# Attention, top-1 experts and FFN on one core: where the routing of three token batches stands among the heads

## The chip, the cores and the metric

One core of a Trainium2 chip runs the whole program. The metric is the device time of one execution in microseconds (us). TensorE (PE), VectorE (DVE), ScalarE (ACT) and GpSimd (POOL) each work through their own list of instructions in order; SyncE (SP) issues most loads and stores. An engine that waits holds up all that stands behind it in its list.

## The reference

Three layers over 4 × 576 = 2304 tokens in fp32: causal attention mixed with a memory read-out (8 heads of 64), a mixture of 8 experts of which each token takes one, and a dense FFN with ELU.

```python
# attention, per batch b and head h
a = softmax(causal(q @ k.T / 8)); local = a @ v
q_p = elu(q) + 1
mem = (q_p @ M_prev) / (q_p @ z_prev + 1e-6)
x = g * mem + (1 - g) * local            # g = sigmoid(beta); heads side by side: 512 wide
# experts
logits = x @ w_gate + modality_bias[modality_id]
e = argmax(logits); gate = softmax(logits)[e]
y = gate * (relu(x @ w1[e]) @ w2[e])     # 512 -> 1024 -> 512
# FFN
out = elu(y @ w_in) @ w_out              # 512 -> 2048 -> 512
```

## The kernel before

Attention runs over 16 pairs of heads (p = 0 to 15; four pairs are one batch of 576 tokens), each in 7 units (k = 0 to 6) of score tiles. One loop walks all units: it issues the scores of a unit on TensorE and then whatever `put(p, k, ...)` has hung on that unit: transposed weights, products with v, the memory's products, loads. So the order of each engine's list is written out by hand, by the numbers of `put` and the constants at the head of the file.

Small VectorE work isn't hung on a unit directly but queued, and `pump()`, called after each scores' minimum, each copy of transposed weights and each step of the feature map, lets out one entry of `steps` and one of `slow` (two of `slow` from the last batch of this loop on, `rate`). `steps` takes a pair's finishing: reciprocals, scaling, and `fin(p)` (L586), which adds memory and local part: four additions a pair, of the main rows (128 x 4 x 128), of the last 64 rows of the batch (`xt`, 64 x 128), and of the two tiles of logits that were computed beside them (widths 8 instead of 64). A batch has 576 = 4 × 128 + 64 tokens; the 64 of an even batch lie in the lower half of `xt`'s partitions, those of an odd batch in the upper half (`rows.start` is 64). L606 sends an addition to VectorE from pair 13 on, or where the rows are the upper half; all others go to GpSimd.

`slow` takes the routing. Tokens are routed in groups of 9, 4 and 5 tiles of 128 (`GROUPS`). For each: `logits` sums the heads' logits, `soft` takes maximum and exponential, `choose` makes the one-hot `oh` and its running sum `r_up` on VectorE and then three products on TensorE (L678 to L680, `tri` and `ones` against `oh` and `r_up`) that count how many tokens of each expert stand before a token; `gates` makes the gate and stores the rows to `xd` in DRAM; `place_a` and `place_b` turn counts into places (`rpi`); `route_d` scatters token numbers to these places in the list `idreg`, by one indirect DMA of GpSimd per tile (L94). `RY` empty entries stand between `choose` and `gates`.

The first two groups are routed in the loop of heads. The first expert is then known; its weights are loaded and split into a high and a low part (`wsplit`, L882 on ScalarE and L883), and `gather0(0)` fetches the first block of 256 rows (`xb`) by the list so far. In the loop's last part stand `scale` (the gate times the rows, L902 on ScalarE and L903 on VectorE) at unit 10 after the last pair's start and `turn` (8 transposes on TensorE, L912, and the split of the result) at unit 13. Block 0 follows: 8 hidden tiles of 12 products (L929), then 4 × 24 products to the output (L948). The last group is routed inside block 0: `logits`, `soft`, `choose` behind hidden tile 0 (`RA`), `gates`, the placements and the five scatters behind tile 2 (`RB`). After hidden tile 7 tables of the experts' counts are made, the second block's list is loaded (`gi`, L886) and its rows are gathered (L888); then 18 scatters fill `idc`, the list of the rows of all later blocks.

Of the kernel before, what the change touches and what calls it, by code (L numbers as in the profile page):

```python
# [10 lines left out]
F32 = mybir.dt.float32  # L11
# [11 lines left out]
E, FF = 8, 1024  # L23
# [3 lines left out]
BLK = 256  # L27
# [27 lines left out]
FINV = 13  # L55
# [5 lines left out]
GB = 7  # L61
EL = (7, 7)
ML = (7, 7)
RA = 0
RB = 2
GK = (5, 5, 5)
SY = 4
RY = 4
# [1 line left out]
MW = (7, 7, 8, 8)  # L70
WSP = (2, 3, 6, 7)
WEN = 'pppp'
SC0 = 10
TU = (13, 13)
H1 = ()
PRE0 = (2, 4)

CD, CQ, CH, CX = S, S + 128, S + 640, S + 768
# [136 lines left out]
def attention(tc, G, ap, hd):  # L215
# [372 lines left out]
    def fin(p):  # L588
        b, hp = p // 4, p % 4
        xs, xt = XS[b % 2], XT[b // 2]  # L590
        if hp == 0:
            nc.gpsimd.memset(xs[:, :, DM + 1 : ROW], 0.0)
            if b % 2 == 0:
                nc.gpsimd.memset(xt[:, DM + 1 : ROW], 0.0)
        c0 = 128 * hp
        mm, ol = MM[p % 2], OL[p % 2]
        r = 64 * (b % 2)
        hs = slice(2 * hp, 2 * hp + 2)
        half = slice(r, r + 64)
        for out, rows, c, d in (  # L600
            (xs[:, :, c0 : c0 + 128].rearrange("p c (j d) -> p c j d", d=64), slice(0, 128), slice(0, 4), slice(0, D)),
            (xt[half, c0 : c0 + 128].rearrange("p (j d) -> p j d", d=64), half, 4, slice(0, D)),
            (LX[:, :, hs], slice(0, 128), slice(0, 4), slice(D, DL)),
            (LT[b // 2][half, hs], half, 4, slice(D, DL)),
        ):
            if p >= FINV or rows.start:  # L606
                steps.append(lambda out=out, rows=rows, c=c, d=d: nc.vector.tensor_tensor(out, mm[rows, c, :, d], ol[rows, c, :, d], op=ALU.add))
            else:
                nc.gpsimd.tensor_tensor(out, mm[rows, c, :, d], ol[rows, c, :, d], op=ALU.add)
# [49 lines left out]
    def choose(t0, K):  # L659
        eq = wk.tile([128, 9, E], F32, tag="r_eq", bufs=1, name=f"r_eq{t0}")[:, :K]  # L660
        fm = wk.tile([128, 9, 1], F32, tag="r_fm", bufs=1, name=f"r_fm{t0}")[:, :K]
        up = wk.tile([128, E * 9], F32, tag="r_up", bufs=1, name=f"r_up{t0}")[:, : E * K]
        L, mxl, O = lg[:, t0 : t0 + K, :], G.gm[:, t0 : t0 + K], oh[:, t0 * E : (t0 + K) * E]
        Oe = O.rearrange("p (e c) -> p e c", e=E)
        nc.vector.tensor_tensor(eq, L, mxl.to_broadcast([128, K, E]), op=ALU.is_equal)
        yield
        nc.vector.tensor_tensor(eq, eq, revE.unsqueeze(1).to_broadcast([128, K, E]), op=ALU.mult)
        yield
        nc.vector.tensor_reduce(fm, eq, axis=AX.X, op=ALU.max)
        yield  # L670
        nc.vector.tensor_tensor(Oe, fm[:, :, 0].unsqueeze(1).to_broadcast([128, E, K]), revE.unsqueeze(2).to_broadcast([128, E, K]), op=ALU.is_equal)
        yield

        nc.vector.tensor_tensor_scan(out=up, data0=G.go[:, t0 * E : (t0 + K) * E], data1=O, initial=0.0, op0=ALU.mult, op1=ALU.add)
        yield
        pt = s(f"r_ps{t0}")[:, 0 : 10 * E]
        pl, al = RT[t0, "pt"] = pt[:, 0 : E * K], pt[:, E * K : E * K + E]
        nc.tensor.matmul(pl, tri, O, start=True, stop=False)  # L678
        nc.tensor.matmul(pl, ones, up, start=False, stop=True)
        nc.tensor.matmul(al, ones, up[:, K - 1 :: K], start=True, stop=True)  # L680
        yield
# [70 lines left out]
    def put(p, k, f, *a):  # L752
        beside.setdefault(NU * p + k, []).append((f, a))
# [41 lines left out]
    for b, (t0, K) in enumerate(((0, 0), (0, 9), (9, 4))):  # L795
# [7 lines left out]
        put(p, k, slow.append, iter((None,) * RY))  # L803
        put(p, k, slow.append, gates(b))
        if K:
            put(p, k, slow.append, place_a(t0, K))
            if b == 2:
                put(p, k, slow.append, first_expert())
# [17 lines left out]
        put(NP - 1, WSP[q], lambda q=q: G.wsplit(0, 0, q, WEN[q], G.RAW0[q]))  # L826
    put(NP - 1, EAR, early)
    put(NP - 1, EAR, lambda: G.gather0(0))
    put(NP - 1, SC0, lambda: G.first_rows())
    put(NP - 1, SC0, lambda: G.scale(G.XB[0]))  # L830
    put(NP - 1, W2L, second_loads)
    put(NP - 1, TU[0], drain)
    for a in range(2):
        put(NP - 1, TU[a], lambda a=a: G.turn(G.XB[0], (a,), G.X0, s))
    for f, k in enumerate(H1):
        put(NP - 1, k, lambda f=f: G.hidden(0, f, G.X0))


    def first_prep(n):
# [15 lines left out]
    while steps or slow:  # L855
        pump()

    ts = range(13, 18)
    G.last_batch = dict(ts=ts, logits=logits(3), soft=soft(3), choose=choose(13, 5), gates=gates(3), place_a=place_a(13, 5), place_b=place_b(13, 5), route_d=route_d)


def define_experts(tc, G):
# [137 lines left out]

def experts(tc, G, mp):
    nc, ct = tc.nc, G.ct
    L = G.last_batch
    oh, rk, run, iotE, cpi = G.oh, G.rk, G.run, G.iotE, G.cpi
    wload, wsplit, gather0, gather1, scale, turn, block = G.wload, G.wsplit, G.gather0, G.gather1, G.scale, G.turn, G.block
    t8 = lambda n: ct(n, [128, E])
# [55 lines left out]
    def start_of(u, j):  # L1062
        return nc.values_load(nxti[0:1, u, j : j + 1], engines=[mybir.EngineType.SP], min_val=0, max_val=NTOK, **why)

    ts = L["ts"]
    P = lambda f, *a: (lambda: f(*a))
    R_ = lambda n: (lambda: deque(L[n], maxlen=0))
    mid1 = {
        RA: [R_("logits"), R_("soft"), R_("choose")],
        RB: [R_("gates"), R_("place_a"), R_("place_b")] + [P(L["route_d"], t) for t in ts],  # L1070
    }
    mid2 = {0: [G.late_T], 1: []}

    def early_load(q):
# [14 lines left out]
    mid2.setdefault(EB[0], []).append(P(early_bits, 0))  # L1089
    mid2.setdefault(EB[1], []).append(P(scale, G.XB[1]))  # L1090
    mid2.setdefault(TX, []).append(P(turn, G.XB[1]))
    block(0, slice(0, BLK), mid1, mid2, len(H1), G.X0)
    W[2][0] = G.kp.tile([128, 4096], F32R, tag="k1", name="W20")
    load_eid(1)
    gather0(2)
# [385 lines left out]
```

## Time and profile before

| | |
|---|---|
| time, median of 3 runs | 971.13 us (970.19 to 972.72) |
| the profiled execution | 980.77 us, of which its span 979.0 |
| mean granted clock of TensorE | 0.95 of full |
| TensorE busy | 891.9 us (91%) |
| VectorE, ScalarE, GpSimd busy | 554.2, 486.6, 279.8 us |
| attention up to its last output product | 258.74 us of the span |
| block 0 and what follows, experts, FFN | from there to 979 us |

How to read it: TensorE is busy nearly always, so time is lost where it isn't, or where it runs at a lower granted clock. The rows further down give busy times by stretches of the span; where a stretch ends with a pair of heads, it is the start of that pair's last product with v (L522).

### The profile page before, as it was taken

How to read it: one execution, taken by the hardware profiler on the slowest of the kernel's cores; microseconds unless marked ns; L12 is line 12 of the kernel's file. 1: busy time of each engine (PE TensorE's matmuls, PEld its weight loads, DVE VectorE, ACT ScalarE, POOL GpSimd, SP SyncE). 2: the span in 40 equal slices, each digit the busy share in tenths (PEclk: the TensorE clock that was granted, in tenths of full speed). 3: DMA queues.
4: the chain of work that ended last, by engine and by line, in shares of the span. 5: the costliest groups of instructions: out<-in, count | busy, mean ns of one | idle time of the engine just before them, and what ended most of it. 6: DMA issues, size and time to landing. Idle time of an engine off the chain costs nothing. (4 is left out here: it accounts for less than half of the span.)

```text
span 979.0 us, 16337 instructions
## 1 busy us (share of the span) xinstructions
PE 891.9 (91%) x6038; PEld 801.3 (82%) x6038; DVE 554.2 (57%) x1280; ACT 486.6 (50%) x1141; POOL 279.8 (29%) x405
## 2 busy tenths in 40 slices
PE   6999988789687899889997689999999999999996
PEld 4887776677676899889995488999999999999995
DVE  7789886688663432244221379888554444644442
ACT  4577765465421222233112365666766666665553
POOL 6443322724326330001100033222332222322223
PEclk7899998898897899989998889999999999999998
DMA  7122322524316160042011033431010000100001
GB/s 185 50 82 85 128 63 102 59 57 143 108 56 159 15 216 23 4 130 88 24 30 36 10 131 134 148 122 72 11 55 1 1 1 1 66 1 1 1 1 64
DMA packets 29553, 65.14 MB, mean 67 GB/s; under 512 B 11008, under 2 KB 11136, under 8 KB 29440
## 3 DMA queue, kind: packets, MB, share of 16 engines
q1 hardware_dynamic: 23520, 49.50, 17.1%
q0 software_dynamic: 4832, 12.14, 4.0%
q10 hardware_dynamic: 1088, 2.10, 0.6%
q8 instruction: 58, 0.95, 0.5%
q14 instruction: 55, 0.45, 0.2%
HBM read 54.14 MB, written 9.58 MB: 65 GB/s over the span
## 5 line engine op out<-in xcount | busy, mean ns | idle before, releaser
L1331 POOL TENSOR_TENSOR gl<-eg,gh 128x384 fp32r<-128x384 f32 x86 | 94.2, 1096 | 274.5 <-PE fh L1312 186.6
L1342 PE MATMUL facc<-wl,gh 128*128 128x512 f32 x288 | 112.6, 391 | 1.0 <-POOL wl L1292 1.0
L1342 PE MATMUL facc<-wh,gl 128*128 128x512 f32 x288 | 112.6, 391 | 0.0
L1342 PE MATMUL facc<-wh,gh 128*128 128x512 f32 x288 | 112.3, 390 | 0.0
L948 PE MATMUL acc<-hs,W 128*128 128x256 f32 x864 | 107.3, 283 | 2.3 <-issue 1.3
L929 PE MATMUL h<-xh,W 128*128 128x256 f32 x512 | 97.4, 292 | 12.6 <-issue 9.1
L948 PEld LDWEIGHTS acc<-hs,W 128*128 128x128 f32 x864 | 104.2, 189 | 3.2 <-ACT hs L931 1.1
L1312 PE MATMUL fh<-yh,first_w 128*128 128x384 f32 x384 | 100.2, 342 | 5.7 <-ACT yh L1303 5.7
L1319 ACT ACTIVATE er<-fh 128x384 f32<-128x384 f32 x96 | 47.2, 492 | 113.1 <-PE fh L1312 110.2
L1322 DVE SCALAR_TENSOR_TENSOR ee<-ee,er 128x384 f32<-128x384 f32 x48 | 27.9, 580 | 120.2 <-ACT er L1321 118.7
L455 ACT ACTIVATE sr<-sr,mx 128x512 f32<-128x512 f32 (+3 forms) x128 | 71.8, 563 | 46.3 <-DVE mx L404 43.7
L929 PEld LDWEIGHTS h<-xh,W 128*128 128x128 f32 x512 | 83.3, 199 | 13.2 <-issue 9.4
L931 ACT ACTIVATE hs<-h 128x256 fp32r<-128x256 f32 x72 | 27.3, 385 | 118.8 <-PE h L929 101.5
L385 POOL TENSOR_TENSOR heads<-lqk,heads 128x704 fp32r<-128x704 f32 (+1 forms) x31 | 46.1, 1488 | 122.9 <-ACT heads L382 107.9
L888 POOL DMA_INDIRECT xb<-xd,gi x26 | 25.3, 973 | 190.1 <-ACT xh L913 77.8
L1312 PEld LDWEIGHTS fh<-yh,first_w 128*128 128x128 f32 x384 | 71.5, 192 | 7.8 <-ACT yh L1303 5.2
L404 DVE CUSTOM_DVE_ANT_0 sr<-s,mb 128x512 f32<-128x512 f32 (+2 forms) x144 | 69.8, 504 | 12.5 <-PE s L436 5.4
L929 PE MATMUL h<-xl,W 128*128 128x256 f32 x256 | 75.0, 293 | 0.3 <-issue 0.3
L932 DVE SCALAR_TENSOR_TENSOR hs<-h,hs 128x256 fp32r<-128x256 f32 x72 | 30.1, 423 | 72.4 <-ACT hs L931 67.0
L489 DVE COPY aT<-t 128x512 f32<-128x512 f32 (+3 forms) x106 | 49.9, 481 | 30.5 <-PE t L477 28.5
L1312 PE MATMUL fh<-yh,wh 128*128 128x384 f32 x192 | 64.5, 336 | 0.9 <-DVE eg L1323 0.9
L1312 PE MATMUL fh<-yh,wl 128*128 128x384 f32 x192 | 64.4, 336 | 0.1
(343 smaller groups left out, 2019.1 us busy)
## 6 DMA issues: line engine op xcount, KB each, us to landing
raw<-in_w_dram SPq DMA_DIRECT2D x20, 512.0 KB
lqk<-in_qk_dram SPq DMA_DIRECT2D x15, 672.0 KB
fraw<-in_win_dram SPq DMA_DIRECT2D x14, 512.0 KB
fraw<-in_wout_dram SPq DMA_DIRECT2D x14, 512.0 KB
vt<-in_vP_dram SPq DMA_DIRECT2D x16, 320.0 KB
xd<-early_rows SPq DMA_DIRECT2D x2, 1032.0 KB
xd<-late_rows SPq DMA_DIRECT2D x2, 1032.0 KB
raw<-in_w_dram ACTq DMA_DIRECT2D x4, 512.0 KB
```

Of the source, the lines that this page charges most:

```text
L385: eng.tensor_tensor(heads[:, p % 2, 1, PART[n]], LD[p % 2][:, PART[n]], heads[:, p % 2, 0, PART[n]].bitcast(F32), op=ALU.subtract)
L404: nc.vector.tensor_tensor_reduce(out=dst, in0=src, in1=mask, scale=-0.125, scalar=start, op0=ALU.add, op1=ALU.min, accum_out=least)
L455: nc.scalar.activation(sr[:, o : o + W], sr[:, o : o + W], AF.Exp, scale=-1.0, bias=mx[:, r : r + 1], accum_out=SUM[p][:, i, j : j + 1])
L489: nc.vector.tensor_copy(dst, src)
L929: nc.tensor.matmul(hp, wt[:, k, 128 * f : 128 * f + 128], xt[:, k, :], start=(k == 0 and r == 0), stop=(k == 3 and r == 2))
L932: nc.vector.scalar_tensor_tensor(hl, hp, 0.0, hh.bitcast(F32), op0=ALU.max, op1=ALU.subtract)
L948: nc.tensor.matmul(o, wt[:, f, 128 * dc : 128 * dc + 128], ht, start=(f == 0 and r == 0), stop=(f == FF // 128 - 1 and r == 2))
L1312: nc.tensor.matmul(hp, wt[:, k, :], xt[:, k, :], start=(k == 0 and r == 0), stop=(k == 3 and r == 2))
L1319: nc.scalar.activation(r, hp, AF.Relu, scale=-1.0)
L1322: nc.vector.scalar_tensor_tensor(e, e, 1.0, r, op0=ALU.add, op1=ALU.mult)
L1331: eng.tensor_tensor(gl, gg, gh.bitcast(F32), op=ALU.subtract)
L1342: nc.tensor.matmul(ACC[g][a], gt[:, c], wt, start=(f == 0 and r == 0), stop=(f == NF - 1 and r == 2))
```

## The change

Three things. In `fin` the condition on the upper half goes: pairs 4 to 7 and 12 now add these rows on GpSimd. The three counting products leave `choose` for a function of their own, `count`, which stands behind `gates`, with `RY` empty entries between it and `place_a`. The last group is routed right after the loop of heads, ahead of `first_rows`, `scale` and `turn` of block 0, all at once; nothing of it is left in block 0. The constants `RA`, `RB`, `SC0`, `TU` and `H1` go.

```diff
@@ fin
-            if p >= FINV or rows.start:
+            if p >= FINV:
                 steps.append(lambda ...: nc.vector.tensor_tensor(out, mm[rows, c, :, d], ol[rows, c, :, d], op=ALU.add))
             else:
                 nc.gpsimd.tensor_tensor(out, mm[rows, c, :, d], ol[rows, c, :, d], op=ALU.add)
@@ choose
         nc.vector.tensor_tensor_scan(out=up, data0=G.go[:, t0 * E : (t0 + K) * E], data1=O, initial=0.0, op0=ALU.mult, op1=ALU.add)
         yield
+
+    def count(t0, K):
+        O, up = oh[:, t0 * E : (t0 + K) * E], RT[t0, "up"]
         pt = s(f"r_ps{t0}")[:, 0 : 10 * E]
         pl, al = RT[t0, "pt"] = pt[:, 0 : E * K], pt[:, E * K : E * K + E]
         nc.tensor.matmul(pl, tri, O, start=True, stop=False)
@@ routing of the first two groups
         put(p, k, slow.append, gates(b))
         if K:
+            put(p, k, slow.append, count(t0, K))
+            put(p, k, slow.append, iter((None,) * RY))
             put(p, k, slow.append, place_a(t0, K))
@@ end of the attention
-    put(NP - 1, SC0, lambda: G.first_rows())
-    put(NP - 1, SC0, lambda: G.scale(G.XB[0]))
     put(NP - 1, W2L, second_loads)
-    put(NP - 1, TU[0], drain)
-    for a in range(2):
-        put(NP - 1, TU[a], lambda a=a: G.turn(G.XB[0], (a,), G.X0, s))
...
     while steps or slow:
         pump()

-    ts = range(13, 18)
-    G.last_batch = dict(ts=ts, logits=logits(3), soft=soft(3), choose=choose(13, 5), gates=gates(3), ...)
+    for f in (logits(3), soft(3), choose(13, 5), count(13, 5), gates(3), place_a(13, 5), place_b(13, 5)):
+        deque(f, maxlen=0)
+    for t in range(13, 18):
+        route_d(t)
+    G.first_rows()
+    G.scale(G.XB[0])
+    G.turn(G.XB[0], (0, 1), G.X0, s)
@@ block 0
-    mid1 = {
-        RA: [R_("logits"), R_("soft"), R_("choose")],
-        RB: [R_("gates"), R_("place_a"), R_("place_b")] + [P(L["route_d"], t) for t in ts],
-    }
+    mid1 = {}
```

The lists of the engines show where this puts things. The second group's counts on TensorE, before, in pair 14 (`s` are scores, `t` transposed weights, `m` the memory's products, `da` and `db` the last products of an earlier pair, `r_ps` the counts):

```order
L477 MATMUL t_2847<-ident,sr_125 128x128 x3
L678 MATMUL r_ps_2856<-oh,tri 128x32
L679 MATMUL r_ps_2856<-r_up_2834,ones 128x32
L680 MATMUL r_ps_2856<-r_up_2834,ones 128x8
L436 MATMUL s_2862<-heads 128x512
L436 MATMUL s_2863<-heads 128x512
L436 MATMUL s_2862<-heads 128x512
L436 MATMUL s_2863<-heads 128x512
```

The same stretch now:

```order
L472 MATMUL t_2847<-ident,sr_125 128x128 x3
L431 MATMUL s_2858<-heads 128x512
L431 MATMUL s_2859<-heads 128x512
...
L431 MATMUL s_2859<-heads 128x512
L472 MATMUL t_2868<-ident,sr_122 128x128 x3
L472 MATMUL t_2885<-ident,sr_123 128x128 x3
L574 MATMUL m_0_2890<-bd,qp_129 128x146 x3
L677 MATMUL r_ps_2900<-oh,tri 128x32
L678 MATMUL r_ps_2900<-r_up_2834,ones 128x32
L679 MATMUL r_ps_2900<-r_up_2834,ones 128x8
L431 MATMUL s_2906<-heads 128x384
```

The counts stand two units later, behind three more scores and transposes and the memory's first products. The first group's counts move in the same way, from behind the scores of the fourth unit of a pair to behind those of the second unit of the next.

TensorE at the end of the attention, before (`pt` is the last pair's output, `t_0` and `t_1` the transposes of block 0's rows, `h_0` its first hidden tile):

```order
L521 MATMUL pt_3290<-aT_128,vt_121 64x64 x10
L522 MATMUL pt_3290<-st_3134,small 128x2
L912 MATMUL t_0_3319<-ident,xb_3209 128x128 x4
L912 MATMUL t_1_3326<-ident,xb_3209 128x128 x4
L546 MATMUL da_3333<-late_rows,oT_134 128x144 x3
L546 MATMUL db_3334<-late_rows,oT_134 128x144 x2
L929 MATMUL h_0_3376<-x_68,W_104 128x256
...
L678 MATMUL r_ps_3406<-oh,tri 128x40
L679 MATMUL r_ps_3406<-r_up_3400,ones 128x40
L680 MATMUL r_ps_3406<-r_up_3400,ones 128x8
L929 MATMUL h_1_3410<-x_68,W_104 128x256
```

The same end now:

```order
L516 MATMUL pt_3287<-aT_128,vt_121 64x64 x10
L517 MATMUL pt_3287<-st_3134,small 128x2
L541 MATMUL da_3316<-late_rows,oT_134 128x144 x3
L541 MATMUL db_3317<-late_rows,oT_134 128x144 x2
L677 MATMUL r_ps_3344<-oh,tri 128x40
L678 MATMUL r_ps_3344<-r_up_3338,ones 128x40
L679 MATMUL r_ps_3344<-r_up_3338,ones 128x8
L911 MATMUL t_0_3375<-ident,xb_3209 128x128 x4
L911 MATMUL t_1_3382<-ident,xb_3209 128x128 x4
L928 MATMUL h_0_3419<-x_68,W_104 128x256
```

The transposes stood ahead of `da` and `db` and now stand behind them and behind the counts, which were between the first and the second hidden tile.

VectorE at the same place, now (`ol` the last pair's scaled local part, `r_...` the routing; before, `xb`, which waits for the gathered rows, stood ahead of both `ol`):

```order
L669 SCALAR_TENSOR_TENSOR r_up_3338<-go,oh 128x40
L635 TENSOR_REDUCE r_sm_3348<-r_ex_3332 128x5
L641 RECIPROCAL late_rows<-r_sm_3348 128x4
L644 RECIPROCAL late_rows<-r_sm_3348 128x1
L686 TENSOR_TENSOR r_rb_3356<-r_ps_3344,run 128x40
L688 TENSOR_TENSOR run<-r_ps_3344,run 128x8
L693 TENSOR_TENSOR r_rb_3356<-r_rb_3356,oh 128x40
L695 TENSOR_REDUCE rk<-r_rb_3356 128x5
L697 CAST rpi<-rk 128x5
L902 TENSOR_SCALAR xb_3209<-xb_3209 128x512
```

The placement is complete before the rows are scaled.

## Rows read from the trace of the kernel before

**Rows 1.** Windows by stage: us, busy time of each engine, clock, DMA share, GB/s.
```profile
core 0: us, PE busy (x) PEld busy (x) DVE busy (x) ACT busy (x) POOL busy (x), PEclk, DMA share, GB/s
60.06:85.13 25.07, 25.07 (x254) 20.77 (x250) 21.99 (x76) 18.81 (x58) 10.17 (x12) 1.00 0.26 83
85.13:141.87 56.74, 51.28 (x505) 41.75 (x501) 49.37 (x166) 37.97 (x118) 18.37 (x17) 1.00 0.28 92
141.87:162.57 20.70, 17.66 (x135) 14.19 (x132) 14.05 (x48) 9.85 (x30) 5.21 (x8) 0.84 0.16 50
162.57:211.15 48.58, 42.09 (x379) 33.47 (x375) 34.07 (x122) 28.65 (x88) 25.43 (x36) 0.93 0.46 92
211.15:231.52 20.37, 16.44 (x135) 13.36 (x132) 15.78 (x56) 9.68 (x31) 4.62 (x6) 0.83 0.20 69
231.52:258.74 27.22, 24.47 (x231) 20.86 (x227) 19.83 (x57) 18.84 (x55) 14.92 (x13) 0.94 0.44 150
258.74:284.64 25.90, 17.89 (x125) 17.66 (x123) 16.54 (x48) 7.67 (x17) 4.47 (x9) 0.87 0.26 91
284.64:345.00 60.36, 47.81 (x339) 45.14 (x338) 26.45 (x65) 10.81 (x21) 26.69 (x52) 0.86 0.35 77
```

**Rows 2.** Timeline, upper rows' addition: start us, us, engine, instructions [idle before <-releaser].
```profile
81.44 0.45 POOL L609 TENSOR_TENSOR xt<-mm,ol 64x128 f32<-64x128 f32 x1
...
93.94 0.95 DVE L607 TENSOR_TENSOR xt<-small,ol 64x128 f32<-64x128 f32 x1
...
96.69 0.30 PE L469 MATMUL t42b<-ident,sr 128*128 128x128 f32 x1 [1.38 <-DVE aT L489]
```

**Rows 3.** Timeline of TensorE, the counts of both groups.
```profile
154.31 0.56 PE L678 MATMUL r_ps<-oh,tri 128*128 128x72 f32 x2 [2.65 <-DVE oh L671]
...
218.13 0.41 PE L678 MATMUL r_ps<-oh,tri 128*128 128x32 f32 x2 [1.71 <-DVE oh L671]
...
220.67 0.64 PE L679 MATMUL r_ps<-r_up,ones 128*128 128x32 f32 x2 [2.14 <-DVE r_up L674]
```

**Rows 4.** Timeline of pair 13's additions, with the last pair's.
```profile
240.28 6.27 DVE L607 TENSOR_TENSOR late_rows<-mm,ol 128x512 f32<-128x512 f32 x4
...
241.82 4.69 POOL L883 TENSOR_TENSOR W<-raw,W 128x1024 fp32r<-128x1024 f32 x2
...
247.20 0.33 PE L436 MATMUL s<-heads 64*128 64x128 f32 x1 [1.44 <-DVE mx L404]
248.69 0.95 PE L436 MATMUL s<-heads 64*128 64x128 f32 x11 [1.16 <-DVE mx L404]
...
268.23 1.44 DVE L607 TENSOR_TENSOR late_rows<-mm,ol 128x512 f32<-128x512 f32 x4
```

**Rows 5.** Timeline of the attention's end and block 0's start, then two windows.
```profile
259.38 0.60 ACT L527 COPY oT<-po 128x512 f32<-128x512 f32 x1
...
261.73 0.48 DVE L903 TENSOR_SCALAR xb<-xb 128x512 f32<-128x512 f32 x1 [6.84 <-DMA xb<-xd,gi]
...
263.77 1.94 PE L912 MATMUL t<-ident,xb 128*128 128x128 f32 x8 [4.65 <-DVE rn L582]
265.51 1.65 PE L546 MATMUL da<-late_rows,oT 128*128 128x144 f32 x6
...
267.44 1.67 PE L929 MATMUL h<-x,W 128*128 128x256 f32 x12
272.47 0.39 PE L678 MATMUL r_ps<-oh,tri 128*128 128x40 f32 x2 [3.36 <-DVE oh L671]
...
273.13 11.67 PE L929 MATMUL h<-x,W 128*128 128x256 f32 x84
...
270.04:272.60 2.56, 0.13 (x2) 0.16 (x2) 2.32 (x11) 0.24 (x1) 0.00 (x0) 1.00 0.00 0
278.53:280.10 1.57, 1.57 (x16) 1.57 (x15) 1.19 (x10) 1.12 (x3) 0.00 (x0) 1.00 0.00 0
```

**Rows 6.** Timeline, the second block's list of indices and its first transpose.
```profile
293.16 0.35 SPq L886 DMA_DIRECT2D gi<-idreg  x1
...
301.30 0.47 PE L912 MATMUL t<-ident,xb 128*128 128x128 f32 x1 [2.92 <-ACT xb L902]
```

More of the change, by code (lines that the diff above doesn't have):

```diff
@@ L63 @@
 ML = (7, 7)
-RA = 0
-RB = 2
 GK = (5, 5, 5)
@@ L72 @@
 WEN = 'pppp'
-SC0 = 10
-TU = (13, 13)
-H1 = ()
 PRE0 = (2, 4)
@@ L661, in choose @@
         fm = wk.tile([128, 9, 1], F32, tag="r_fm", bufs=1, name=f"r_fm{t0}")[:, :K]
-        up = wk.tile([128, E * 9], F32, tag="r_up", bufs=1, name=f"r_up{t0}")[:, : E * K]
+        up = RT[t0, "up"] = wk.tile([128, E * 9], F32, tag="r_up", bufs=1, name=f"r_up{t0}")[:, : E * K]
         L, mxl, O = lg[:, t0 : t0 + K, :], G.gm[:, t0 : t0 + K], oh[:, t0 * E : (t0 + K) * E]
@@ L828, in attention @@
     put(NP - 1, EAR, lambda: G.gather0(0))
-    put(NP - 1, SC0, lambda: G.first_rows())
-    put(NP - 1, SC0, lambda: G.scale(G.XB[0]))
     put(NP - 1, W2L, second_loads)
-    put(NP - 1, TU[0], drain)
-    for a in range(2):
-        put(NP - 1, TU[a], lambda a=a: G.turn(G.XB[0], (a,), G.X0, s))
-    for f, k in enumerate(H1):
-        put(NP - 1, k, lambda f=f: G.hidden(0, f, G.X0))
     def first_prep(n):
@@ L856, in attention @@
         pump()
-    ts = range(13, 18)
-    G.last_batch = dict(ts=ts, logits=logits(3), soft=soft(3), choose=choose(13, 5), gates=gates(3), place_a=place_a(13, 5), place_b=place_b(13, 5), route_d=route_d)
+    for f in (logits(3), soft(3), choose(13, 5), count(13, 5), gates(3), place_a(13, 5), place_b(13, 5)):
[5 more added lines that the diff above has]
+    G.turn(G.XB[0], (0, 1), G.X0, s)
 def define_experts(tc, G):
@@ L1002, in experts @@
     nc, ct = tc.nc, G.ct
-    L = G.last_batch
     oh, rk, run, iotE, cpi = G.oh, G.rk, G.run, G.iotE, G.cpi
@@ L1063, in start_of @@
         return nc.values_load(nxti[0:1, u, j : j + 1], engines=[mybir.EngineType.SP], min_val=0, max_val=NTOK, **why)
-    ts = L["ts"]
     P = lambda f, *a: (lambda: f(*a))
-    R_ = lambda n: (lambda: deque(L[n], maxlen=0))
-    mid1 = {
-        RA: [R_("logits"), R_("soft"), R_("choose")],
-        RB: [R_("gates"), R_("place_a"), R_("place_b")] + [P(L["route_d"], t) for t in ts],
-    }
+    mid1 = {}
     mid2 = {0: [G.late_T], 1: []}
@@ L1091, in experts @@
     mid2.setdefault(TX, []).append(P(turn, G.XB[1]))
-    block(0, slice(0, BLK), mid1, mid2, len(H1), G.X0)
+    block(0, slice(0, BLK), mid1, mid2, 0, G.X0)
     W[2][0] = G.kp.tile([128, 4096], F32R, tag="k1", name="W20")
```

## The prediction

> **What bounds the kernel now.** I read the windows by stage first. The cuts are the ends of the head pairs' output products on TensorE, so a stage of n pairs should last n times one pair. The first row is what a pair costs when nothing disturbs it: two pairs in 25.07 us with TensorE busy all the time at full granted clock, so 12.53 us a pair [rows 1]. The bound is TensorE, and every stage longer than its pairs times 12.53 holds waits or a lower clock. The excess of the stages is: four pairs in 56.74 (6.6 over), one pair in 20.70 (8.2 over), three pairs in 48.58 (11.0 over), one pair in 20.37 (7.8 over), two pairs in 27.22 (2.2 over). Then come the end of the attention with the first block's hidden tiles (25.90, TensorE busy 17.89) and the rest of block 0 with what follows it (60.36, busy 47.81). Where TensorE is busy less than the stage, its clock is lower too (0.83 to 0.87). So about 36 us of excess lie in the attention [rows 1], and the change acts at three places of it and at the two stages behind it. Second I read, at each place, the wait of TensorE and what ended it [rows 2 to 6].
>
> **Upper additions to GpSimd (pairs 4 to 7 and 12).** VectorE loses ten additions, GpSimd gains them. The undisturbed stage is one in which GpSimd already does all four additions of a pair; the stage of four pairs in 56.74 is the one where two of them are VectorE's. There the addition of the upper rows took 0.95 on VectorE, and once a pair TensorE waits 1.38 us for a copy of transposed weights that stands behind it on VectorE; the same addition took 0.45 on GpSimd [rows 2]. Four such waits are 5.5 us. Bounds: the whole excess, 6.6, if these pairs become as short as the undisturbed ones; 5.5 − 4 × 0.45 = 3.7 if GpSimd's extra addition holds VectorE up for its length. GpSimd is busy 18.37 of 56.74 there, so it doesn't become the bound [rows 1]. I take 5.5, since the undisturbed stage has the very same work on GpSimd. Pair 12 lies in a stage that the next items cover; nothing extra is taken for it.
>
> A rule speaks against this part: the undisturbed stage, two pairs with all additions on GpSimd, has TensorE at 25.07 of 25.07 [rows 1], but the Trainium skill (SBUF — State Buffer, "SBUF: two separate sides") says that VectorE and GpSimd share a pair of ports as an exclusive lock, the loser of which stands still for the whole instruction, and names VectorE operations with two SBUF inputs among the contenders. Four VectorE additions of 1.44 that took 6.27 beside a GpSimd subtraction of 4.69 [rows 4] agree with it. By the rule the work only changes the engine that holds the lock, and this item would fall to the 3.7 of the lower bound.
>
> **First batch's counts.** The three products for the ranks of tokens 0 to 8 (`r_ps`) stood right behind `choose`; TensorE, which works in order, waited there 2.65 us for the one-hot on VectorE [rows 3]. They now stand after `gates` and four empty steps, in the next pair by the order: VectorE's operands are then long done, so this wait can't recur. The stage is 8.2 over; its clock, 0.84, makes up to 0.16 × 17.66 = 2.8 of that, and I hold the clock for a consequence of the waits. What limits the gain is VectorE: it is busy 14.05 in the stage, so the pair can't be shorter than that, which leaves at most 6.65 [rows 1]. The two placement steps, moved into the next pair, fall on a VectorE that is busy 11 us of a pair's 12.53 (21.99 for two) [rows 1], so they fit. I take 3.5 (the wait and a third of the clock's part); bounds 1, if the scores' waits on VectorE take the place of the wait, and 6.
>
> The nine scatters of this batch hang on `place_b` and go out one pair later, from pair 12 on instead of 11. Both pairs lie in the stage of 48.58, whose 11.0 us of excess holds their burst before and after [rows 1]; I take 0, bounds −4 and 4.
>
> **Second batch's counts.** Here TensorE waited twice, 1.71 for the one-hot and 2.14 for the running sums [rows 3], 3.85 in all, in a stage of 20.37 with VectorE busy 15.78; VectorE caps the gain at 4.6 [rows 1]. I take 3.5; bounds 1 and 4.6. The cast for the scatters comes four empty steps later, at two steps a pump two pumps, of which a pair has 19 in the code: 2 × 12.53 / 19 = 1.3 us, an estimate; four scatters stand on GpSimd before its subtraction for the expert's weights, so that moves back too. That subtraction of 4.69 us ran beside the four additions of pair 13 on VectorE, which took 6.27 instead of the 1.44 that the same four took for the last pair, and two scores products waited 1.44 and 1.16 behind them [rows 4]. If the subtraction starts 1.3 us later the additions pass it; these 2.6 us go. Bounds 0 (still beside it) and 4.8 (6.27 − 1.44). I take 2.6.
>
> **Last batch ahead of block 0.** Before, VectorE's scaling of the gathered rows stood in front of the last pair's additions: VectorE idle 6.84 for the gather, TensorE 4.65 behind it until the transposes at 263.77; then, after the first hidden tile (1.67 us from 267.44), TensorE waited 3.36 more for the last batch's one-hot, and the second tile began at 273.13 [rows 5]. Now nothing waits for the gather, but routing is in series with the transposes. Its length from rows: output copied to SBUF at 259.98; from the first `da` product to the end of the last additions 4.16 (265.51 to 269.67); logits to running sums 2.56; gates and placement 1.57; scaling 0.48 [rows 4, 5]. That is 268.8; transposes 1.94, first tile 1.67, and the second tile begins at 272.4, against 273.13. I take 0.5. Bounds: a loss of 5.0 (transposes at 268.8 instead of 263.77, nothing given back) and a gain of 3, if the additions run in the shadow of the products. The five scatters and their queue on GpSimd are hidden behind the hidden tiles, as GpSimd is busy 4.47 of 25.90 there [rows 1].
>
> **Second block.** Placement of the last batch is over some 12 us earlier (268 instead of 280.10), so its scatters are too, and the list of indices for the second block, loaded at 293.16, can come as much earlier; TensorE waited 2.92 for that block's rows at 301.30 [rows 5, 6]. The lists of later blocks follow by 3 to 5 us only, because the long chain of scatters that they hang on follows the tables. I take 4; bounds 0 and 8, out of the 12.5 us in which TensorE is idle in this stage [rows 1].
>
> **Sum.** 5.5 + 3.5 + 3.5 + 2.6 + 0.5 + 4 = 19.6. The profiled execution took 980.77 with a span of 979.0, 1% above the median of the runs, 971.13; scaled by that, 19.4. So 961.2 for a profiled execution and 971.13 − 19.4 = **951.7** as the time.
>
> **Rivals.**
> - The counts are only moved: for want of VectorE's time, the scores' waits take the place of both waits (stages of 20.70 and 20.37 stay). VectorE is busy 14.05 and 15.78 there, more than a pair's 12.53 [rows 1], which speaks for it; that three quarters of the stage suffices speaks against. 7.0 less gained: 958.6.
> - The routing is fully in series: the second block gains nothing, and the transposes' 5.0 us aren't given back by the 3.36. 9.5 less: 961.1. For it: VectorE's steps of 0.2 each, one behind the other, 2.32 busy of 2.56 [rows 5].
> - More comes back: the clock returns to 1.00 in all four attention stages that were under it; 0.16 × 17.66 + 0.17 × 16.44 + 0.07 × 42.09 + 0.06 × 24.47 = 10 us [rows 1]: 941.
> - Slower: TensorE now has one gap of some 6 us (262 to 268.8) with eight small products in it, where before there were two of 4.65 and 3.36 with work between. If the granted clock then goes to its lower level, 1.2 GHz, and stays, each hidden product costs 0.139 more (84 in 11.67 [rows 5]). It decides from the 142nd product on (19.6 / 0.139), that is if the low clock lasts through all of block 0's 96 hidden products and half its output: 192 at low clock give 971.13 + 7 = 978. Against it: after the gaps of before the 84 products ran at full speed at once.
> - No change: the routing in series, the counts only moved and the additions at their lower bound, with some clock lost: within 0.3%.
>
> **Chances.** Forecast (944 to 957) 0.54; counts only moved 0.14; in series 0.15; more 0.06; no change 0.05; slower 0.06. The range 943 to 963 leaves out the last two, most of the case of more and a part of the series case, about 2 in 10. A difference of 0.3%, 2.9 us, is about what a measurement of this kernel can tell from none. Faster by more 0.89, within 0.05, slower by more 0.06.
>
> **What the profile after would show.** Additions: pairs 4 to 7 in about 51 us instead of 56.74, no wait for `aT` of a microsecond per pair. Counts: no wait of TensorE ahead of `r_ps`; stages of about 17 instead of 20.70 and 20.37. Pair 13: four additions in under 3 us. End: transposes of block 0 at the equivalent of 268 on this time axis and no `r_ps` between hidden tiles; one gap on TensorE, not two. Second block: no wait for `xb` before its transposes. The prediction is wrong if waits for `mx` or score banks of the same length stand where the `r_ps` waits were, if the stages keep their clock of 0.83, or if the gap ahead of block 0 grows past 10 us.

## Result, and the profile after

The changed kernel takes 954.51 us (median of 4 runs, 953.83 to 955.89) against 971.02 for the one before: a ratio of 0.983, 95% interval 0.9811 to 0.9848. The forecast was 951.7 with a range of 943 to 963. On another chip the ratio was 0.982 (0.978 to 0.986).

The windows by stage, cut at the same places as [rows 1] (start of a pair's last product with v, then the first output product of block 0); columns as there:

```profile
core 0: us, PE busy (x) PEld busy (x) DVE busy (x) ACT busy (x) POOL busy (x), PEclk, DMA share, GB/s
85.20:136.02 50.82, 50.71 (x505) 41.75 (x501) 45.11 (x158) 37.83 (x118) 21.00 (x25) 1.00 0.32 102
136.02:152.28 16.26, 13.89 (x129) 10.74 (x126) 14.33 (x48) 9.81 (x30) 5.24 (x8) 1.00 0.21 64
152.28:191.49 39.21, 39.21 (x385) 32.34 (x381) 32.75 (x122) 28.39 (x88) 20.77 (x31) 1.00 0.51 103
191.49:211.30 19.81, 16.45 (x135) 12.93 (x131) 15.18 (x49) 9.82 (x31) 9.53 (x14) 0.91 0.37 91
211.30:236.04 24.74, 23.27 (x232) 19.00 (x228) 17.64 (x69) 17.95 (x54) 9.26 (x10) 1.00 0.50 148
236.04:264.88 28.84, 16.68 (x111) 15.66 (x110) 18.36 (x39) 7.98 (x18) 11.93 (x22) 0.70 0.28 96
264.88:325.00 60.12, 50.20 (x400) 49.56 (x400) 31.12 (x72) 14.35 (x27) 28.04 (x44) 0.91 0.48 114
```

Against [rows 1] the attention's stages give 5.9 (56.74 to 50.82, VectorE's additions gone), 4.4 (20.70 to 16.26, the first group's counts), 9.4 (48.58 to 39.21, a gain that no term of the sum has), 0.6 (20.37 to 19.81, the second group's counts) and 2.5 (27.22 to 24.74, the additions of pair 13). The end of the attention with the first hidden tiles is 2.9 longer. To the first transposes of the second block it comes out 0.7 shorter (301.30 − 258.74 = 42.6 before, 277.88 − 236.04 = 41.8 now), and 2.4 more are gained from there to the FFN's first product (263.1 to 260.7). Without the 9.4 this is 16.5, and the FFN, which the change doesn't touch, was 1.1 shorter; together the 26.9 by which the profiled spans differ (979.0 and 952.1). The medians differ by 16.5. The profile of before (980.77) was no run of the four, which take 970.19 to 972.72; whether the 9.4 belong to the change is a question for the experiments.

The timeline of the changed kernel, rows that answer to [rows 3 to 5] (L669 makes the running sums, L602 the additions, L380 GpSimd's subtraction for `heads`, L882 its weight subtractions, L666 the one-hot, L928 the hidden products):

```profile
197.22 0.52 PE L472 MATMUL t<-ident,sr 128*128 128x128 f32 x3 [0.79 <-DVE aT L484]
...
198.52 0.50 PE L431 MATMUL s<-heads 64*128 64x512 f32 x1 [0.79 <-DVE mx L399]
...
200.83 1.68 POOL L380 TENSOR_TENSOR heads<-lqk,heads 128x704 fp32r<-128x704 f32 x1 [5.12 <-ACT heads L377]
200.93 1.65 DVE L669 TENSOR_TENSOR_SCAN r_up<-go,oh 128x32 f32<-128x32 f32 x1
...
202.64 0.41 PE L678 MATMUL r_ps<-r_up,ones 128*128 128x32 f32 x2 [0.42 <-DVE r_up L669]
...
204.83 0.79 PE L431 MATMUL s<-heads 64*128 64x384 f32 x5 [1.16 <-DVE mx L399]
...
220.65 1.41 DVE L602 TENSOR_TENSOR late_rows<-mm,ol 128x512 f32<-128x512 f32 x4
...
237.55 6.45 DVE L602 TENSOR_TENSOR late_rows<-small,ol 128x512 f32<-128x512 f32 x4
...
238.07 4.64 POOL L882 TENSOR_TENSOR W<-raw,W 128x1024 fp32r<-128x1024 f32 x2
...
245.04 1.44 DVE L602 TENSOR_TENSOR late_rows<-mm,ol 128x512 f32<-128x512 f32 x4
...
248.83 0.24 DVE L669 TENSOR_TENSOR_SCAN r_up<-go,oh 128x40 f32<-128x40 f32 x1
248.94 0.62 PE L677 MATMUL r_ps<-oh,tri 128*128 128x40 f32 x2 [10.12 <-DVE oh L666]
...
253.38 13.26 PE L928 MATMUL h<-x,W 128*128 128x256 f32 x96
```

The waits of 1.71 and 2.14 for the second group's counts have shrunk to 0.42, but TensorE now waits 0.79, 0.79 and 1.16 for minima and copies in the same pair. Pair 13's additions take 1.41 instead of 6.27. Five microseconds of the same sort have turned up at a worse place: pair 14's additions take 6.45 beside GpSimd's last two subtractions, and TensorE stands idle 10.12 us for the last group's one-hot behind them.

### The profile page after: what moved, and what is told of

It is laid out like the page before. It is cut to its first block, busy times and chain, and to the rows that moved or that the text cites. A ratio compares the mean times of both kernels' runs of the same rounds, so it can differ in the third digit from the quotient of the medians.

```text
span 952.1 us, 16341 instructions
## 1 busy us (share of the span) xinstructions
PE 878.4 (92%) x6038; PEld 790.8 (83%) x6038; DVE 549.1 (58%) x1270; ACT 485.5 (51%) x1141; POOL 282.3 (30%) x415
## 3 DMA queue, kind: packets, MB, share of 16 engines
q1 hardware_dynamic: 23520, 49.50, 17.9%
## 5 line engine op out<-in xcount | busy, mean ns | idle before, releaser
L947 PE MATMUL acc<-hs,W 128*128 128x256 f32 x864 | 109.3, 287 | 10.0 <-DVE hs L931 9.9
L947 PEld LDWEIGHTS acc<-hs,W 128*128 128x128 f32 x864 | 106.4, 193 | 10.7 <-DVE hs L931 10.3
L928 PE MATMUL h<-xh,W 128*128 128x256 f32 x512 | 93.7, 285 | 7.2 <-issue 6.9
L928 PEld LDWEIGHTS h<-xh,W 128*128 128x128 f32 x512 | 80.5, 193 | 7.6 <-issue 7.1
L380 POOL TENSOR_TENSOR heads<-lqk,heads 128x704 fp32r<-128x704 f32 (+1 forms) x31 | 46.2, 1489 | 101.6 <-ACT heads L377 85.8
L928 PE MATMUL h<-xl,W 128*128 128x256 f32 x256 | 73.1, 285 | 0.2 <-DVE xl L913 0.2
```

The source lines that it names most:

```text
L380: eng.tensor_tensor(heads[:, p % 2, 1, PART[n]], LD[p % 2][:, PART[n]], heads[:, p % 2, 0, PART[n]].bitcast(F32), op=ALU.subtract)
L928: nc.tensor.matmul(hp, wt[:, k, 128 * f : 128 * f + 128], xt[:, k, :], start=(k == 0 and r == 0), stop=(k == 3 and r == 2))
L947: nc.tensor.matmul(o, wt[:, f, 128 * dc : 128 * dc + 128], ht, start=(f == 0 and r == 0), stop=(f == FF // 128 - 1 and r == 2))
```

## The experiments

Three parts, so the first question is what each is worth alone and in pairs; the second, where the 9.4 come from; the third, whether pair 14's additions are long because of GpSimd. The text calls the long pair around the nine scatters (some 21 us instead of 12.5) the stall. The experiments were timed on three chips, each with its own median of the kernel before: 977.63, 967.67 and 976.85. The pairs' lengths in this section are differences of the start of the last product with v (L522, in the changed kernel L517) of one pair and the next, read from the timeline. The columns: pairs 4 to 7; the pair of the first group's counts; the pair around the nine scatters (one later where the counts are moved); the pair of the second group's counts; the two pairs behind; from there to block 0's transposes (t0); from these to the second block's (t1).

| kernel | ratio to before | 4 to 7 | 1st counts | scatters | 2nd counts | last two | to t0 | t0 to t1 |
|---|---|---|---|---|---|---|---|---|
| before | | 56.7 | 20.7 | 21.5 | 20.4 | 27.2 | 5.0 | 37.5 |
| before, again | | 56.7 | 20.6 | 21.4 | 20.4 | 27.1 | 2.0 | 37.6 |
| additions | 0.991 (0.988 to 0.994) | 50.8 | 20.5 | 21.6 | 19.6 | 27.1 | 2.1 | 37.8 |
| counts | 1.001 (0.997 to 1.005) | 56.7 | 16.0 | 21.0 | 19.2 | 25.2 | 10.3 | 37.5 |
| counts, again | 0.999 (0.996 to 1.002) | 56.7 | 17.7 | 20.9 | 19.3 | 27.0 | 8.0 | 37.1 |
| last group | 0.994 (0.991 to 0.996) | 56.7 | 20.6 | 20.3 | 20.6 | 28.1 | 9.1 | 27.4 |
| additions, counts | 0.994 (0.990 to 0.997) | 50.8 | 17.9 | 12.5 | 20.9 | 24.7 | 11.4 | 39.9 |
| counts, last group | 0.992 (0.989 to 0.996) | 56.8 | 16.0 | 12.5 | 23.0 | 25.0 | 13.6 | 28.2 |
| additions, last group | 0.987 (0.982 to 0.992) | 50.8 | 19.5 | 21.2 | 19.7 | 27.2 | 9.1 | 27.7 |
| all three | 0.983 (0.981 to 0.985) | 50.8 | 16.3 | 12.5 | 19.8 | 24.7 | 14.2 | 27.7 |
| all three, again | 0.982 (0.978 to 0.986) | 50.8 | 16.3 | 21.0 | 18.2 | 25.0 | 13.7 | 28.1 |
| all, eight writes more | 0.987 (0.983 to 0.991) | 51.3 | 17.7 | 12.5 | 20.7 | 25.3 | 10.9 | 27.4 |
| all, subtractions first | 0.978 (0.973 to 0.983) | 50.8 | 16.3 | 12.5 | 22.0 | 25.4 | 9.2 | 26.9 |
| the same, again | 0.980 (0.977 to 0.984) | 50.8 | 16.3 | 22.0 | 16.6 | 29.0 | 9.1 | 28.1 |

**Before, again.** No edit.

> The kernel before once more, for a second profiled execution. The three pairs before the second group's routing took 48.58 us in the first one and 39.21 in the changed kernel, a gain that no term of the prediction has. If those 9 us belong to the one profiled execution (980.77 beside a median of 971), this stage now takes about 40 and the whole about 971. If they belong to the program (the burst of nine scatters one pair earlier), it takes 48 again and the missing 10 us lie elsewhere.

This execution took 974.89. The stall is in it too: 21.4 us for the pair around the scatters. So it isn't a slip of one profile: of the kernels that have their counts where they were, every profiled execution has it (five: 21.5, 21.4, 21.6, 20.3, 21.2), though none of them was taken on the second of the three chips.

**The additions alone.**

```diff
-            if p >= FINV or rows.start:
+            if p >= FINV:
```

> The upper additions on GpSimd alone. Theory of the prediction: 5.5 us less than before (965.5), the stage of four pairs in about 51 us, everything else as before. Rival, the shared ports: additions on GpSimd hold VectorE up in the same way, so 3.7 or less (967.3 or more).

968.92 against 977.63 on this chip, 0.991. The windows of that kernel:

```profile
85.20:136.02 50.82, 50.71 (x504) 41.75 (x500) 45.14 (x158) 37.85 (x118) 20.99 (x25) 1.00 0.32 102
136.02:156.54 20.52, 17.25 (x136) 13.98 (x132) 14.19 (x48) 9.91 (x30) 5.21 (x8) 0.83 0.16 51
```

The first row is the changed kernel's, to the hundredth: 5.9 us less than before and TensorE busy 50.71 of 50.82; the second, the counts' pair, is nearly that of [rows 1]. The 8.7 us of the medians have an interval of 5.5 to 12, which holds the 5.9. The rival's price, 3.7 or less, is out: no 0.45 per pair was lost.

But the two engines do get in each other's way here, in the kernel before. The 0.95 of [rows 2] isn't what this addition costs VectorE. In each of pairs 4 to 7 it ran beside GpSimd's addition of the main rows and ended 0.15 us after it; with no such neighbour the same shape takes VectorE 0.29, as in pair 14 of the changed kernel. First GpSimd's addition in the kernel before, then VectorE's in the changed one:

```profile
93.46 1.28 POOL L609 TENSOR_TENSOR late_rows<-small,ol 128x512 f32<-128x512 f32 x1
...
243.28 0.29 DVE L602 TENSOR_TENSOR late_rows<-small,ol 64x128 f32<-64x128 f32 x1
```

The move pays because one engine now does both additions one behind the other, not because GpSimd is the faster one (0.45 against 0.29).

**The counts alone**, twice.

```diff
+    def count(t0, K):
+        O, up = oh[:, t0 * E : (t0 + K) * E], RT[t0, "up"]
         pt = s(f"r_ps{t0}")[:, 0 : 10 * E]
...
         put(p, k, slow.append, gates(b))
         if K:
+            put(p, k, slow.append, count(t0, K))
+            put(p, k, slow.append, iter((None,) * RY))
             put(p, k, slow.append, place_a(t0, K))
...
-        RA: [R_("logits"), R_("soft"), R_("choose")],
+        RA: [R_("logits"), R_("soft"), R_("choose"), R_("count")],
```

> The counts of the first two groups behind the gates alone, the last group where it was. From the profiles of before and after: 4.4 us of the first group's stage, 0.6 of the second's and 2.5 of pair 13, together 7.5 (963.5). If the counts are what shortens the three-pair stage too, 10 more (954 to 957). Rival, only moved: within 2 us of 971.

> The counts alone, again. Its lists of instructions are the same up to the nine scatters as those of the kernel with counts and last group, which had no stall around them (12.53 us for the pair) where this one had (20.97). If the stall is decided by the single execution, this one shows 12.5 or 21 at random; if by the program, 21 again.

1.001 and 0.999: worth nothing alone, which of the expected numbers only the rival's had. Yet the counts do what they should: from the first pair's last product to the last pair's, the attention takes 214.9 and 218.4 us, against 223.5 in the second profile of before. What is gained, 8.6 and 5.1, is lost right behind: from the attention's end to the second block's transposes 47.8 and 45.1 instead of 39.6, so 8.2 and 5.5. The timeline of the first of the two shows why:

```profile
247.28 0.98 POOL L894 DMA_INDIRECT xb<-xd,gi  x1 [9.86 <-issue]
...
252.10 2.38 DVE L909 TENSOR_SCALAR xb<-xb 128x512 f32<-128x512 f32 x1 [11.78 <-DMA xb<-xd,gi]
...
256.04 1.94 PE L918 MATMUL t<-ident,xb 128*128 128x128 f32 x8 [9.90 <-DVE rn L582]
```

The second group is placed later, and the attention ends sooner, so block 0's rows aren't there: VectorE waits 11.78 for the gather, all else behind it, and TensorE 9.90. A chain of DMAs (scatters, list, gather) that used to be done at about the attention's end now ends well after it: the gather is issued 1.5 us behind the attention's end here, and was issued 6.1 us ahead of it (252.65 of 258.74) in the kernel before.

**The last group alone.** The routing of group (13, 5) and `turn` behind the loop as in the change, with the counts still in `choose`.

```diff
-    put(NP - 1, SC0, lambda: G.first_rows())
-    put(NP - 1, SC0, lambda: G.scale(G.XB[0]))
...
-    for a in range(2):
-        put(NP - 1, TU[a], lambda a=a: G.turn(G.XB[0], (a,), G.X0, s))
...
+    for f in (logits(3), soft(3), choose(13, 5), gates(3), place_a(13, 5), place_b(13, 5)):
+        deque(f, maxlen=0)
+    for t in range(13, 18):
+        route_d(t)
+    G.first_rows()
+    G.scale(G.XB[0])
+    G.turn(G.XB[0], (0, 1), G.X0, s)
```

> The last group ahead of block 0 alone, the counts inside the choice as before. From the profiles: 2.9 lost at the end of the attention, 7.1 gained behind it, so 4.2 us less than before (966.8). If the loss comes from GpSimd's weight subtraction beside the additions of pair 14, and that only happens since the second group is placed later, the end is 5 us shorter here: about 962. Rival, routing in series: 971 or more.

971.40 against 977.63, 0.994. The transposes come 9.1 us after the attention's end instead of 2.0, and the second block's 27.4 us behind them instead of 37.6, without any wait, since its list is ready early: 36.5 against 39.6, 3.0 gained in the trace (6.2 by the medians, 3.9 to 8.8; the rest I can't place). Here pair 14's additions are short and TensorE waits half as long:

```profile
259.59 1.36 DVE L607 TENSOR_TENSOR late_rows<-small,ol 128x512 f32<-128x512 f32 x4
...
265.89 0.62 PE L678 MATMUL r_ps<-oh,tri 128*128 128x40 f32 x2 [5.03 <-DVE oh L671]
```

So the 10.12 of the changed kernel comes about only with the counts moved, as the expectation's second case had it; the time it named, 962, was too low.

**In pairs.** Additions and counts (the two edits above together), counts and last group (the changed kernel with the old condition in `fin`), additions and last group.

> Additions and counts together, the last group left inside block 0. If the nine scatters' stall (8.4 us in the pair around them, in the kernel before, with the additions alone and with the counts alone, but not in the changed kernel) goes only with both, the attention ends as early as in the changed kernel, near 236. Block 0's transposes then wait for their rows as with the counts alone, some 10 us after the attention's end, and block 0 lasts 37.5 instead of 27.7: 4 to 6 us more than the changed kernel, 958.5 to 960.5. Rival: the stall stays, since it needs the last group's move: 967 or more.

> The changed kernel without its additions on GpSimd. If only the waits of pairs 4 to 7 come back: 5.9 us more than the changed kernel, 960.4. If the scatters' stall comes back with them: 8.4 more, about 969.

> The changed kernel without the move of the counts: additions on GpSimd and the last group ahead of block 0. If the counts bring in the whole what the stages show (4.4 in the first group's pair, 8.4 around the scatters, less some 3 to 8 us of waiting for the first block's rows), it takes 5 to 10 us more than the changed kernel. If what the counts give in the attention is given back at its end in full, it takes the same as the changed kernel within 3 us.

963.69, 960.49 (both against 967.67) and 965.06 (against 976.85, where all three take 961.18). Additions and counts: transposes 11.4 after the end and block 0 long, as expected; the time is above what was named, and the 4.0 us gained are less than the additions gained alone (8.7, on another chip). Counts and last group: pairs 4 to 7 long again, and no stall around the scatters; the 960.5 is the number named, but on a chip where the kernel before takes 967.67, so 7.2 us are gained (4 to 11) where some 10.6 were expected. Additions and last group: 3.9 us more than all three on the same chip. There the counts shorten the attention by 7.5 (215.6 to 208.1, first pair's last product to last pair's) and lengthen the way to the second block by 5.0 (36.7 to 41.7): 2.5 are left. The intervals of the two ratios, 0.982 to 0.992 and 0.978 to 0.986, overlap, so the counts' worth on top of the others isn't settled beyond "small".

**Eight tiny writes on VectorE.** The nine scatters go out in every kernel in about 12 us; some executions stall around them and some don't. My theory was that it matters where in VectorE's list of instructions the burst falls, and that VectorE's shorter list moved that place.

```diff
+    G.pad = ct("pad", [1, 1])
...
+    for p in range(4, 8):
+        for k in range(2):
+            put(p, 6, lambda: nc.vector.memset(G.pad, 0.0))
```

> The changed kernel with eight additional one-element writes on VectorE in pairs 4 to 7, where it has eight additions fewer than before; they do nothing and cost VectorE about half a microsecond in a stretch where it has time. If the scatters' stall depends on where in VectorE's list of instructions the burst falls, it comes back: the pair around the nine scatters takes about 21 us instead of 12.5, and the whole about 962. If the stall hangs on the additions themselves (their engine, their timing), nothing changes: 954.5.

The pair took 12.54: no stall, and 957.09. By itself this doesn't settle it, since no execution profiled on this chip has the stall, whatever the kernel. What speaks against the theory is below: lists that are the same, with the stall and without. The windows around the nine scatters in three executions, the counts alone, counts with the last group, and before again:

```profile
180.37:201.34 20.97, 15.44 (x130) 11.67 (x126) 10.75 (x38) 9.73 (x29) 14.35 (x23) 0.92 0.51 50
```

```profile
184.20:196.73 12.53, 12.53 (x129) 10.39 (x126) 11.47 (x37) 9.38 (x29) 10.76 (x19) 1.00 0.74 53
```

```profile
176.90:198.34 21.44, 16.13 (x129) 12.57 (x126) 10.89 (x38) 9.73 (x29) 14.10 (x23) 0.84 0.53 49
```

The first two kernels have the same instructions in the same order on every engine up to the end of the burst. One execution had the stall and the other not. With the counts moved, it was there in four of nine profiled executions (one on the first chip, three on the third) and absent in five (four of them on the second); with the counts in place it was there in all five, and none of these was taken beside the four on the second chip. Sorted by chip the experiments part cleanly: on the first and the third every profiled execution has the stall, four and four, whatever the kernel; on the second none of four has it. The medians of the kernel before differ there in the same sense (977.63 and 976.85 against 967.67). That points at the chip rather than the change, but the two profiles of before and after that this document starts from differ in it too, and no profile of the kernel before without the stall exists. So whether the move of the burst has to do with it stays open. The list of waits in the stalled window of the counts alone names no cause for some of it ("issue" is a wait for nothing that the profile shows, "remote" one that something outside the profile ended):

```profile
ACT sr L450 <- issue: 2.6, 1, 2.6
...
ACT aT L487 <- remote: 1.5, 1, 1.5
...
DVE aT L489 <- remote: 1.2, 1, 1.2
```

**All three, again.** No edit.

> The changed kernel again, timed on the same chip as the three beside it: 0.983 of before, as before. Its pair around the nine scatters takes 12.5 us, if that isn't a matter of the single execution.

0.982, and the profiled execution, 964.89 and the slowest of the four, has the stall (20.97). It is the changed kernel itself, which had 12.53 in its first profile, so the program alone doesn't decide it. Pair 14's additions:

```profile
245.61 5.93 DVE L602 TENSOR_TENSOR late_rows<-small,ol 128x512 f32<-128x512 f32 x4
...
256.48 0.62 PE L677 MATMUL r_ps<-oh,tri 128*128 128x40 f32 x2 [9.60 <-DVE oh L666]
```

**Subtractions ahead of the gather**, twice. In the changed kernel GpSimd waits 7.65 us for the gather's indices with two weight subtractions queued behind it.

```diff
-WSP = (2, 3, 6, 7)
+WSP = (2, 3, 5, 5)
```

> The changed kernel with the last two weight subtractions of GpSimd ahead of its gather for block 0 instead of behind it. In the changed kernel the gather waits 7.65 us for its indices, the subtractions (4.64) start behind it at 238.07, and the four additions of pair 14 on VectorE take 6.45 beside them instead of 1.44, with the last group's routing and block 0's transposes behind. If the two engines keep each other out there, the additions now take 1.4, the transposes begin 5 us earlier and the time is 949.5. If something else holds the additions up, 954.5.

> The changed kernel with GpSimd's last two weight subtractions ahead of its gather, again, beside the changed kernel on the same chip: 5 us less than that.

949.48 against 967.67, 0.978, and 958.13 against 976.85, 0.980; beside the changed kernel on the same chip 3.1 us less (956.8 to 960.2 and 957.0 to 964.9, so not clear of each other). The timeline of the first:

```profile
225.22 9.45 POOL L882 TENSOR_TENSOR W<-raw,W 128x1024 fp32r<-128x1024 f32 x4
...
239.96 1.36 DVE L602 TENSOR_TENSOR late_rows<-small,ol 128x512 f32<-128x512 f32 x4
...
241.11 0.98 POOL L887 DMA_INDIRECT xb<-xd,gi  x1 [6.44 <-DMA gi<-idreg]
...
246.33 0.62 PE L677 MATMUL r_ps<-oh,tri 128*128 128x40 f32 x2 [5.10 <-DVE oh L666]
```

All four subtractions run back to back, the gather still waits for its indices, the additions take 1.36 instead of 6.45 and TensorE's wait falls from 10.12 to 5.10. The same instructions, another neighbour: it was GpSimd's subtractions that held VectorE up. Taken one by one, a single addition bears the whole delay each time: the first of the four in the changed kernel (5.72), the second when it ran again (4.87), the last, of 64 x 16, in pair 13 of the kernel before (5.03):

```profile
237.55 5.72 DVE L602 TENSOR_TENSOR late_rows<-small,ol 128x512 f32<-128x512 f32 x1
```

```profile
246.25 4.87 DVE L602 TENSOR_TENSOR late_rows<-small,ol 64x128 f32<-64x128 f32 x1
```

```profile
241.52 5.03 DVE L607 TENSOR_TENSOR late_rows<-mm,ol 64x16 f32<-64x16 f32 x1
```

Each is recorded as starting just ahead of the first subtraction (238.07, 246.31, 241.82) and ends just behind the second (242.71, 250.96, 246.51). The transposes come 9.2 after the attention's end instead of 14.2. Of the 5 us some are lost ahead: the conversions on ScalarE now stand in front of exponentials, and the second run's TensorE waited longer for a copy by ScalarE in the last pair (1.10 in the changed kernel on that chip):

```profile
241.52 3.69 PE L509 MATMUL po<-aT,vt 128*64 128x128 f32 x16 [2.76 <-ACT aT L482]
```

## Why the prediction came out right, step by step

**Additions: right, for a reason the prediction had the wrong way round.** 5.5 forecast, 5.9 measured, alone and with the others. The undisturbed stage with the same work on GpSimd was the right row to go by. But the prediction took 0.95 for VectorE's own price of this addition, and the shared ports for a rule that speaks against the move. The 0.95 was 0.29 and a wait for GpSimd; the move took that meeting away.

**The first group's counts: right.** 3.5 forecast, 4.4 in the stage (2.8 to 4.7 in the other kernels that move them); the granted clock went from 0.84 to 1.00 with the wait gone, as the prediction held.

**The second group's counts: the term that was mis-sized.** 3.5 forecast, 0.6 measured, below the bound of 1. The step that failed is that the two waits just go: they shrank to 0.42, and waits of 0.79, 0.79 and 1.16 for minima and copies took their place, with VectorE busy 15.18 of 19.81. This was the rival "only moved", true for one group and not for the other. One reason can be read from the rows: of the 2.14 for the running sums, 1.4 was a meeting with GpSimd. The scan that makes these sums took 1.65 beside GpSimd's subtraction for `heads`, and takes 0.24 for the last group, where it has no such neighbour. Before:

```profile
218.87 1.67 POOL L385 TENSOR_TENSOR heads<-lqk,heads 128x704 fp32r<-128x704 f32 x1 [8.64 <-ACT heads L382]
...
218.97 1.65 DVE L674 TENSOR_TENSOR_SCAN r_up<-go,oh 128x32 f32<-128x32 f32 x1
```

In the changed kernel the scan meets the same subtraction again (200.93, also 1.65). So VectorE still loses 1.4 us there, and TensorE now waits for a minimum (the 1.16) that stands behind the scan. A run that moves the scan off the subtraction would show what that alone is worth; there is none.

**Pair 13: right.** 2.6 forecast, 2.5 measured; the additions fell to 1.41, since GpSimd's subtractions (two, 4.69 together, which the prediction calls one) began at 223.44 only.

**The end of the attention: the place was right, the price too low.** The transposes were forecast 10.1 us after the attention's end (268.8 − 258.74) and came after 14.2. The 4.1 are pair 14's additions, 5 us longer beside the subtractions; subtractions ahead of the gather took them off. I had that collision in [rows 4], for pair 13, and moved GpSimd's work past it without asking what it would meet next. That shared ports make this so is what the Trainium skill (SBUF — State Buffer, "SBUF: two separate sides") says of a VectorE operation with two SBUF inputs beside a GpSimd one that reads SBUF: the one that starts first holds the pair for its whole instruction, and the other stands still. The 6.45, 5.93 and 1.36 agree with the standing still, and so do the 0.95 of pairs 4 to 7 and the scan's 1.65. They don't agree with who wins: by the records the addition had started 0.06 to 0.52 us ahead of the subtraction, and it waited through two of them. By the prediction's own sign, a gap ahead of block 0 of more than 10 us (10.12), this part was wrong.

**The second block: right in its mechanism.** Forecast 0.5 and 4 for the end and the second block together; measured 0.7 to the second block's transposes and 2.4 behind them, 3.1 in all. Between the two sets of transposes 9.8 were gained (37.5 to 27.7), which the end gave back. Split where the prediction splits it, at the second hidden tile, both terms lie outside their bounds: that tile starts 20.4 us after the attention's end instead of 14.4, so 6.0 are lost, where a gain of 0.5 was forecast and a loss of 5.0 was the bound. Behind it 6.7 are gained up to the second block's transposes and 2.4 after them, together 9.1, where 4 was forecast and 8 was the bound. That the two nearly cancel as forecast is luck. And it hangs on the profile: in the second profile of before the transposes come only 2.0 after the end, and against that one the way to the second block is 2.3 longer and the way to the FFN's first product 0.5 longer (302.0 to 302.5).

**The burst of scatters:** 0 forecast, 9.4 in the two profiles, and not shown to be an effect of the change: the changed kernel's second profile has the stall too.

**Slower:** the rival of the lower clock came in part, and cost nothing beyond what the kernel before paid. The gap of 10 us is there, the stage's mean granted clock fell from 0.87 to 0.70, and the lower of the two levels (1.2 GHz) stayed through the counts, the transposes and the first 14 hidden products; then the higher one (2.4 GHz) came back. But all 96 hidden products took 13.26 us, against 1.67 and 11.67 in [rows 5], since there the lower level had come too, in the midst of the 84. So these didn't run "at full speed at once", as the prediction says. First the changed kernel, then the one before, columns as in [rows 1]:

```profile
239.72:256.79 17.07, 6.71 (x28) 6.00 (x29) 11.86 (x31) 2.37 (x6) 7.31 (x12) 0.50 0.26 85
256.79:264.88 8.09, 8.09 (x71) 8.09 (x70) 4.20 (x7) 4.68 (x9) 1.26 (x9) 1.00 0.01 0
```

```profile
273.96:277.38 3.42, 3.42 (x19) 3.42 (x18) 0.42 (x1) 0.39 (x1) 0.00 (x0) 0.50 0.00 0
277.38:284.64 7.26, 7.26 (x64) 7.26 (x63) 5.95 (x15) 4.57 (x8) 3.60 (x7) 1.00 0.54 182
```

From the start of one hidden product to the next it is 0.118 us at 1.00 and 0.213 at 0.50, so the lower level costs 0.095 each and not the 0.139 of the prediction, which is a mean over both.

**More:** three of the four stages that this rival names did go back to a clock of 1.00 (the fourth to 0.91), but the only gain there beyond the terms above is the 9.4.

The forecast of 19.6 less the errors (additions +0.4, first counts +0.9, second −2.9, pair 13 −0.1, end and second block −1.4) is 16.5. Three terms were within a microsecond; the sum came out 3 too high. That it equals the difference of the medians is chance: by the second profile of before the same stages give 12.7, and some 4 of the medians' 16.5 then stay unplaced. And the terms aren't independent, as the sum has them: the counts, with pair 13 forecast at 9.6, are worth nothing alone and some 3.9, not clear of the noise, on top of the other two parts, where the additions alone bring 8.7 and the last group alone 6.2.

## What to carry to other kernels

A wait taken out of the middle brings the end nearer, and with it whatever was just in time: here the gather of the next stage's rows, which gave back all that the moved counts had gained until another part put work in front of it. Changes in one pipeline are worth what they are worth together; alone the counts brought nothing, and beside the last group's move a little. When work of an engine is moved past a collision, look for the next instruction that it will stand beside: two subtractions on GpSimd cost four additions on VectorE 5 us, first in pair 13, then in pair 14. And before a time in a profile is taken for an instruction's price, look for the same shape elsewhere in the trace: an addition of 0.95 that takes 0.29 without its neighbour, and a scan of 1.65 that takes 0.24, are waits.

## What the runs showed of the hardware

Some VectorE instructions with two inputs in SBUF stood still beside additions and subtractions on GpSimd, until these were over: an addition of 64 x 128 took 0.95 to 1.02 instead of 0.29 beside one addition, a running-sum scan 1.65 instead of 0.24 beside one subtraction, and a single addition 4.87 to 5.72 instead of 0.17 to 0.69 beside two subtractions in a row.

The pair around nine indirect scatters, which take 12 us of GpSimd's time, was 8 to 9.5 us longer in some executions and not in others, with identical lists of instructions up to there; VectorE and ScalarE then stand idle without a releaser in the profile (2.6, 1.5 and 1.2 us, ended by "issue" or "remote"). Where the stall is absent, the pair behind is longer (19.8 to 23.0 us against 16.6 to 19.3), so that its net price is some 7 us: for all three parts the scatters' pair and the three behind it take 57.1 without and 64.2 with it, and with the subtractions ahead of the gather 59.9 and 67.5. What decides it wasn't found.
